# Hash attention with a gated feed-forward: head pairs, exponentials as the stationary operand, a feature-major hash in column tiles, token-major outputs

## Chip, cores and metric

One core of one Trainium2 chip. The metric is the device time of one execution in microseconds (us). Each kernel was executed four to eight times per batch, always beside the kernel before on the same chip. Most executions of one kernel agree within 1.5%; one that is over 1.5% above the fastest of its kernel is marked slow, and only the others ("fast runs") are compared. The clock in this text is the TensorE clock that the profile records as granted, as a share of full speed; in the records it is 1.0 or 0.5, and other values are means over a stretch. At full clock matmuls of 512 columns start 216 ns apart, or some 2.4 columns a nanosecond (written 2.4 GHz below).

## The reference, cut to what matters

```python
q, k, v: [4, 8, 768, 64] * 0.1      # batch, heads, sequence, head dimension
proj:    [64, 6]                    # hash projection
q_bits = (q @ proj > 0);  k_bits = (k @ proj > 0)          # 6 bits each
mask   = bucket(q_bits)[:, :, :, None] == bucket(k_bits)[:, :, None, :]
scores = where(mask, q @ k^T / 8, -1e9)
attn   = softmax(scores);  attn_out = attn @ v
x      = attn_out as [3072, 512]
ffn    = (gelu(x @ w_gate) * (x @ w_val)) @ w_out          # w_gate, w_val: [512, 1536]
out    = x + sigmoid(x @ w_res) * ffn
```

Both kernels compute the mask inside the score matmul: the 64 features of a query or key get hash rows appended, so that a mismatch in a bit makes the score so negative that its exponential vanishes.

## The kernel before, the parts that matter

```python
# per head and side: transposes, hash, signs, transposed back as rows
for t in range(ST):
    nc.tensor.transpose(ap[:D, bass.ts(t, 128)], ten_s[:, t, :], ident)          # L104, fp32
for (n0, nsz) in NCH:                                                            # (0, 512), (512, 256)
    nc.scalar.copy(ten_aug[0:D, n0:n0 + nsz], ap[:D, n0:n0 + nsz])               # L106
for t in range(ST):
    nc.tensor.matmul(bp[:, t * NBITS:(t + 1) * NBITS],
                     ten_aug[0:D, bass.ts(t, 128)], proj_sb, ...)                # L109: loads 128 columns, streams 6
nc.scalar.activation(sgn[:, :], bp[:, :ST * NBITS], AF.Sign)
for t in range(ST):
    nc.tensor.transpose(sp[:NBITS, bass.ts(t, 128)], sgn[:, t, :], ident_bf)     # L116
nc.scalar.copy(ten_aug_bf[D:KAUG, :], sp[:NBITS, :S])                            # L117
# ... cut ...
# per head: values stationary, exponentials streamed; output is feature-major
for jt in range(ST):
    for (n0, nsz) in NCH:
        sp = score_psum.tile([128, 512], FP32, tag="sp")                         # 2 single-bank buffers
        nc.tensor.matmul(sp[:, :nsz], k_aug_bf[0:KAUG, bass.ts(jt, 128)],
                         q_aug_bf[0:KAUG, n0:n0 + nsz], ...)                     # L134
        nc.scalar.activation(e[:, n0:n0 + nsz], sp[:, :nsz], AF.Exp,
                             scale=exp_scale, bias=exp_bias_sb)                  # L138
    for (ot, n0, nsz) in ots:
        nc.tensor.matmul(ot[:, :nsz], v_aug[:, jt, :], e[:, n0:n0 + nsz], ...)   # L141
for (ot, n0, nsz) in ots:
    nc.vector.reciprocal(recip[0:1, n0:n0 + nsz], ot[D:D + 1, :nsz])             # L148: one partition
nc.gpsimd.partition_broadcast(recip[:, :], recip[0:1, :])
# ... x = ot * recip, then: weights loaded and cast, feed-forward,
#     feature-major output transposed back to rows (L222, L223) ... cut ...
```

The softmax here doesn't subtract the row's maximum and nothing guards it: scores larger than these inputs give would overflow.

## Time and profile before

| | before |
|---|---|
| time, four executions of the batch that timed the change | median 800.62 us (793.58 to 805.14) |
| span of the profiled execution | 793.3 us |
| attention (to about 535 us), mean clock | 0.66 from 24 to 533 us |
| feed-forward with weight load and tail | about 258 us |

The groups by shape that the change touches, beyond the views that the prediction quotes (line, engine, operation, out<-in, shapes, count | busy us, mean ns of one | idle time of the engine just before, and what ended it):

```profile
L138 ACT ACTIVATE e<-sp,exp_bias_sb 128x512 bf16<-128x512 f32 x192 | 131.9, 687 | 61.6 <-PE sp L134 57.3 <-PE ap L104 0.7
L148 DVE RECIPROCAL recip<-ot 1x512 f32<-1x512 f32 x32 | 107.3, 3352 | 141.9 <-PE ot L141 141.9
L141 PE MATMUL ot<-e,v_aug 128*65 128x512 bf16 x192 | 104.2, 543 | 26.8 <-ACT e L138 26.8
L109 PE MATMUL bp<-proj_sb,q_aug 64*128 64x6 f32 x384 | 71.7, 316 | 1.5 <-ACT q_aug L106 1.5
```

The hash group L109 (twice: this one for queries, a like one for keys) streams six columns per matmul. The profile lists every fp32 matmul except transposes as two records, so the 768 records of L109 are 384 matmuls of the program; no sum here depends on it. A reciprocal of one partition takes 3.35 us for 512 columns. These 32 take 107 us of VectorE, and 162 us with the 32 of 256 columns (54.8 us, not shown), though most of it beside other work.

### The profile page before, as it was taken

Reading aid. Unit: us, or ns where it says so; the run is one execution under the profiler, and the core shown is the slowest. Engines: PE = TensorE matmul, PEld = TensorE weight load, DVE = VectorE, ACT = ScalarE, POOL = GpSimd, SP = SyncE. Lnnn points to the kernel's source line nnn. Section 1 sums busy time; section 2 is a strip of 40 time slices with the busy share of each in tenths; the row PEclk is TensorE's granted clock in tenths of the full one; section 3 lists DMA queues with packets and bytes.
Section 4 is the critical chain, followed back from the end, with each engine's and each line's share of the span. In section 5 each row is a group of like instructions: output and inputs, shape, how many; then the busy total and the mean of one; then the engine's idle time right before and its main releaser. Section 6 shows DMA issues by size and latency. Waiting matters only on the chain.

```text
span 793.3 us, 8913 instructions
## 1 busy us (share of the span) xinstructions
PE 712.2 (90%) x3360; PEld 412.1 (52%) x3360; DVE 325.4 (41%) x383; ACT 409.0 (52%) x845; POOL 37.5 (5%) x40
## 2 busy tenths in 40 slices
PE   3999998899998899998899998773889999999995
PEld 3666665566665566665556664330334444444442
DVE  1033434633346554444564335545524243333331
ACT  1465556755567675556665655550333343445341
POOL 0000000100001010000100000010000000000000
PEclk9965557865567785557675655555899999999997
DMA  8211111111111121111111000008531010101001
GB/s 141 58 40 41 40 41 30 41 41 40 40 40 39 32 51 40 40 41 30 40 31 31 0 1 1 0 0 283 154 85 61 1 54 0 54 12 43 32 22 54
DMA packets 82299, 36.24 MB, mean 46 GB/s; under 512 B 76112, under 2 KB 76112, under 8 KB 82256
## 3 DMA queue, kind: packets, MB, share of 16 engines
q1 hardware_dynamic: 82256, 35.66, 17.3%
q8 instruction: 27, 0.44, 0.2%
q14 instruction: 16, 0.13, 0.1%
HBM read 29.36 MB, written 6.29 MB: 45 GB/s over the span
## 4 chain that ended last, share of the span: by engine, by line
PE 78%; ACT 10%; issue 6%; DMA 4%; DVE 2%; ACTq 0%; POOL 0%; DVEq 0%; POOLq 0%
PE bp L109 17%; PE ot L141 13%; PE ap L104 10%; PE sp L134 10%; PE fps L213 7%; PE gps L191 7%; PE vps L197 7%; ACT e L138 5%; PE sp_raw L116 5%; DMA tmp<-in_moe_w_out_dram 3%; PE rps L205 2%; ACT k_aug_bf L117 2%; DMA out_dram<-o_row 1%; PE tp L222 1%; ACT q_aug_bf L117 1%
## 5 line engine op out<-in xcount | busy, mean ns | idle before, releaser
L138 ACT ACTIVATE e<-sp,exp_bias_sb 128x512 bf16<-128x512 f32 (+1 forms) x384 | 206.8, 577 | 61.6 <-PE sp L134 57.3
L148 DVE RECIPROCAL recip<-ot 1x512 f32<-1x512 f32 x64 | 160.9, 2532 | 141.9 <-PE ot L141 141.9
L141 PE MATMUL ot<-e,v_aug 128*65 128x512 bf16 (+1 forms) x384 | 166.4, 458 | 26.8 <-ACT e L138 26.8
L134 PE MATMUL sp<-q_aug_bf,k_aug_bf 70*128 70x512 bf16 (+1 forms) x384 | 153.6, 454 | 0.0
L194 ACT ACTIVATE gtmp<-gps 128x512 bf16<-128x512 f32 x72 | 42.9, 597 | 109.8 <-PE gps L191 109.2
L191 PE MATMUL gps<-x_sb,t 128*128 128x512 bf16 x288 | 81.0, 392 | 11.4 <-DVE t L169 9.8
L134 PEld LDWEIGHTS <-k_aug_bf 70*128 70x128 bf16 x384 | 50.3, 131 | 71.8 <-issue 61.3
L197 PE MATMUL vps<-x_sb,t 128*128 128x512 bf16 x288 | 78.5, 389 | 5.8 <-DVE t L169 5.8
L109 PEld LDWEIGHTS bp<-proj_sb,q_aug 64*128 64x128 f32 x384 | 68.8, 271 | 17.5 <-ACT q_aug L106 17.1
L199 DVE TENSOR_TENSOR hh<-gtmp,vps 128x512 bf16<-128x512 bf16 x72 | 49.3, 687 | 69.1 <-PE vps L197 59.9
L141 PEld LDWEIGHTS <-v_aug 128*65 128x65 bf16 x384 | 56.4, 147 | 38.9 <-issue 23.5
L109 PE MATMUL bp<-proj_sb,q_aug 64*128 64x6 f32 x384 | 71.7, 316 | 1.5 <-ACT q_aug L106 1.5
L109 PEld LDWEIGHTS bp<-proj_sb,k_aug 64*128 64x128 f32 x384 | 61.1, 244 | 17.7 <-ACT k_aug L106 17.7
L213 PE MATMUL fps<-hh,t 128*128 128x512 bf16 x288 | 64.7, 382 | 4.3 <-DVE t L169 4.2
L109 PE MATMUL bp<-proj_sb,k_aug 64*128 64x6 f32 x384 | 64.0, 296 | 1.6 <-ACT k_aug L106 1.6
L112 ACT ACTIVATE sgn_t<-bp 128x36 bf16<-128x36 f32 x64 | 12.8, 200 | 94.6 <-PE bp L109 94.6
L149 POOL PARTITION_BROADCAST recip<-recip x32 | 36.4, 1137 | 495.6 <-DVE recip L148 495.6
L104 PE MATMUL ap<-ident,q_s 128*64 128x128 f32 x192 | 46.7, 403 | 14.5 <-POOL ident masks.py:199 9.0
L121 DVE CAST k_aug_bf<-k_aug 64x768 bf16<-64x768 f32 x32 | 18.0, 562 | 83.4 <-ACT k_aug L106 83.4
L191 PEld LDWEIGHTS <-t 128*128 128x128 bf16 x288 | 27.6, 100 | 43.0 <-issue 8.8
L104 PE MATMUL ap<-ident,k_s 128*64 128x128 f32 x192 | 46.7, 405 | 3.4 <-ACT q_aug_bf L117 3.4
L197 PEld LDWEIGHTS <-t 128*128 128x128 bf16 x288 | 27.9, 99 | 40.8 <-DVE t L169 10.1
(34 smaller groups left out, 473.0 us busy)
## 6 DMA issues: line engine op xcount, KB each, us to landing
q_s<-in_q_dram SPq DMA_DIRECT2D x32, 192.0 KB, 2.6
k_s<-in_k_dram SPq DMA_DIRECT2D x32, 192.0 KB, 2.6
v_tmp<-in_v_dram SPq DMA_DIRECT2D x32, 192.0 KB, 3.0
out_dram<-o_row SPq DMA_DIRECT2D x24, 256.0 KB, 2.0
tmp<-in_moe_w_gate_dram SPq DMA_DIRECT2D x4, 768.0 KB, 4.2
tmp<-in_moe_w_val_dram SPq DMA_DIRECT2D x4, 768.0 KB, 4.2
tmp<-in_moe_w_out_dram SPq DMA_DIRECT2D x12, 256.0 KB, 2.7
tmp<-in_moe_w_res_dram SPq DMA_DIRECT2D x4, 256.0 KB, 2.7
```

The costliest lines, as they stand in the source:

```text
L104: nc.tensor.transpose(ap[:D, bass.ts(t, 128)], ten_s[:, t, :], ident)
L109: nc.tensor.matmul(bp[:, t * NBITS:(t + 1) * NBITS], ten_aug[0:D, bass.ts(t, 128)], proj_sb, start=True, stop=True)
L116: nc.tensor.transpose(sp[:NBITS, bass.ts(t, 128)], sgn[:, t, :], ident_bf)
L134: nc.tensor.matmul(sp[:, :nsz], k_aug_bf[0:KAUG, bass.ts(jt, 128)], q_aug_bf[0:KAUG, n0:n0 + nsz], start=True, stop=True)
L138: nc.scalar.activation(e[:, n0:n0 + nsz], sp[:, :nsz], AF.Exp, scale=exp_scale, bias=exp_bias_sb)
L141: nc.tensor.matmul(ot[:, :nsz], v_aug[:, jt, :], e[:, n0:n0 + nsz], start=(jt == 0), stop=(jt == ST - 1))
L148: nc.vector.reciprocal(recip[0:1, n0:n0 + nsz], ot[D:D + 1, :nsz])
L191: nc.tensor.matmul(gps, wg[:, kk, bass.ts(m, P)], x_bf[:, kk, :], start=(kk == 0), stop=(kk == KM - 1))
L194: nc.scalar.activation(gtmp, gps, AF.Gelu)
L197: nc.tensor.matmul(vps, wv[:, kk, bass.ts(m, P)], x_bf[:, kk, :], start=(kk == 0), stop=(kk == KM - 1))
L199: nc.vector.tensor_mul(hh[:, m, :], gtmp, vps)
L213: nc.tensor.matmul(fps, wo[:, kk, bass.ts(m, P)], hh[:, kk, :], start=(kk == 0), stop=(kk == KF - 1))
```

## The change

Its intent: take the narrow matmuls out of attention and make every output come out in the layout that its consumer wants.

- Two heads share one fp32 transpose. The hash becomes one wide fp32 matmul per side and half, with the projection stationary and the tokens streamed; the four sides of two pairs write to four column tiles (partitions 0, 32, 64, 96). A comparison gives the bits, and small transfers copy them under the features.
- Scores of 1024 columns (two banks, filled from head and key tiles without gaps) get one exponential. The exponentials are the stationary operand of the value matmul: 65 columns are streamed (64 values and a one for the sum), and tokens come out in partitions. A reciprocal is then 128 x 6. One matmul per head adds a tiny epsilon times the sum of all values, for rows without a match.
- Feed-forward weights are loaded during attention and cast on GpSimd. The last matmuls use the hidden tile as the stationary operand, so rows come out ready to store. The sigmoid becomes a tanh.

```diff
-                    for t in range(ST):
-                        nc.tensor.matmul(bp[:, t * NBITS:(t + 1) * NBITS],
-                                         ten_aug[0:D, bass.ts(t, 128)], proj_sb, ...)
-                    nc.scalar.activation(sgn[:, :], bp[:, :ST * NBITS], AF.Sign)
-                    ... sign transposes, copy of the rows ...
+            for (t0, n) in CH:
+                hs = misc_ps.tile([P, 512], FP32, tag="m", name="hs")
+                for pi in range(2):
+                    for side in range(2):
+                        j = 2 * pi + side
+                        nc.tensor.matmul(hs[32 * j:32 * j + 32, :n * P], projw,
+                                         t32[pi, side][:, t0 * P:(t0 + n) * P], ...)      # L166
+                nc.vector.tensor_scalar(bits[:, t0 * P:(t0 + n) * P], hs[:, :n * P], 0.0, cst,
+                                        op0=ALU.is_gt, op1=ALU.add)                       # L169
... preparation of a pair's side: transposes L137, evacuation L139, casts to the two heads:
+                    nc.gpsimd.tensor_copy(ag[0:D, :, 0, :], t3[0:D])                      # L144
+                    nc.vector.tensor_copy(ag[0:D, :, 1, :], t3[D:2 * D])                  # L145
... value copies L150 and sums L154 to L157 on GpSimd ...
-                        nc.tensor.matmul(ot[:, :nsz], v_aug[:, jt, :], e[:, n0:n0 + nsz], ...)
+                sp = sc_ps.tile([P, 1024], FP32, tag="sp", name="sp")                     # 2 buffers of two banks
+                ... score matmuls into sp ...                                             # L212
+                e = e_pool.tile([P, 1024], BF16, tag="e", name="e")
+                nc.scalar.activation(e, sp, AF.Exp, scale=float(ALPHA))                   # L217
+                        nc.tensor.matmul(o, eps_sb, vsum[...], start=True, stop=False)    # L223
+                        for qt in range(qt0, qt0 + nq):
+                            nc.tensor.matmul(av[hi][:, qt, :], e[:, off:off + P],
+                                             va[:, hi, jt, 0:D + 1], ...)                 # L230
-                    nc.vector.reciprocal(recip[0:1, n0:n0 + nsz], ot[D:D + 1, :nsz])
-                nc.gpsimd.partition_broadcast(recip[:, :], recip[0:1, :])
+                nc.vector.reciprocal(rec, o[:, :, D])                                     # L201
... feed-forward ...
-                nc.scalar.activation(res[:, m, :], rps, AF.Sigmoid)
+                nc.scalar.activation(th, rps, AF.Tanh, scale=0.5)
+                    nc.tensor.matmul(fps, hh[:, m, bass.ts(tt, P)], wo[:, m, :], ...)
-            ... 16 transposes and 16 copies per row tile, then the store ...
+                nc.sync.dma_start(out_t[row // T, row % T], o)
```

## The prediction

> **What bounds the kernel now.** I read the page first (engines, slices, chain), then the groups by shape, then stretches and the order of time.
>
> ```profile
> PE 712.2 (90%) x3360; PEld 412.1 (52%) x3360; DVE 325.4 (41%) x383; ACT 409.0 (52%) x845; POOL 37.5 (5%) x40
> PEclk9965557865567785557675655555899999999997
> PE 78%; ACT 10%; issue 6%; DMA 4%; DVE 2%; ACTq 0%; POOL 0%; DVEq 0%; POOLq 0%
> PE bp L109 17%; PE ot L141 13%; PE ap L104 10%; PE sp L134 10%; PE fps L213 7%; PE gps L191 7%; PE vps L197 7%; ACT e L138 5%; PE sp_raw L116 5%; DMA tmp<-in_moe_w_out_dram 3%; PE rps L205 2%; ACT k_aug_bf L117 2%; DMA out_dram<-o_row 1%; PE tp L222 1%; ACT q_aug_bf L117 1%
> ```
>
> TensorE is the bound, and for two thirds of the span it runs at a granted clock of 0.5 to 0.8. The costliest line of the chain is not attention: it is the hash projection L109, 17% of 793 us = 135 us, for 768 matmuls of six columns. Transposes L104 (79 us) and sign transposes L116 (40 us) are preparation too.
>
> By stretches of time (columns: stretch, its length, busy us of PE, PEld, DVE, ACT, POOL with counts, clock, DMA share, GB/s):
>
> ```profile
> 160.00:220.00 60.00, 58.48 (x286) 39.29 (x285) 22.94 (x27) 34.92 (x72) 3.25 (x3) 0.61 0.18 40
> 460.00:535.00 75.00, 63.06 (x222) 32.91 (x222) 34.48 (x31) 41.57 (x82) 5.24 (x5) 0.52 0.00 0
> 535.00:565.00 30.00, 13.25 (x34) 3.57 (x35) 16.05 (x19) 3.56 (x5) 1.56 (x1) 0.54 0.71 237
> 615.00:780.00 165.00, 163.59 (x798) 75.39 (x796) 53.84 (x76) 67.27 (x145) 0.00 (x0) 1.00 0.07 26
> 780.00:793.00 13.00, 3.69 (x19) 1.49 (x17) 1.92 (x2) 3.47 (x16) 0.00 (x0) 0.68 0.22 82
> ```
>
> So: attention to 535 us; some 17 us of idle PE from 535 to 565 while feed-forward weights load and are cast; feed-forward at full clock from about 565 to 780; a tail of 13 us, transposing and storing the last rows.
>
> The order of time gives what one matmul really costs, from start to start (durations of single matmuls overlap):
>
> ```profile
> 63.11 0.80 PE L116 MATMUL sp_raw<-ident_bf,sgn_t 128*6 128x128 bf16 x6
> 64.79 1.49 PE L104 MATMUL ap<-ident,q_s 128*64 128x128 f32 x6
> 66.07 0.85 PE L141 MATMUL ot<-e,v_aug 128*65 128x512 bf16 x2
> 66.71 0.85 PE L134 MATMUL sp<-q_aug_bf,k_aug_bf 70*128 70x512 bf16 x2
> 67.49 2.73 PE L109 MATMUL bp<-proj_sb,q_aug 64*128 64x6 f32 x12
> ...
> 76.76 0.50 PE L116 MATMUL sp_raw<-ident_bf,sgn_t 128*6 128x128 bf16 x6
> ```
>
> At clock 0.5 (64 to 74 us), 768 columns of scores take 66.71 to 67.35 = 0.64 us, twelve hash matmuls 2.65 us, six transposes 64.79 to 66.07 = 1.28 us, or 213 ns each. At clock 1.0 (76 to 77.7 us) the sign transposes fall from 122 to 56 ns (single starts in the trace), while fp32 transposes take 213 ns in both stretches. Feed-forward matmuls of 512 columns at full clock are 216 ns apart.
>
> **What the Trainium skill says.**
> - "TensorE: Matmul & The Clock Gate", Part 1: the clock is half or full, set by activity in windows of about 3.4 us, and an idle window brings it down. The trace agrees on two levels and on 3.4 us pieces. But PE has no idle of that length at 160 to 220 us (58.5 busy of 60) and the clock still falls; it falls after windows holding twelve L109 matmuls, which load weights and stream almost nothing. I read the gate as counting streamed columns: counting starts per window, it rises after windows with at most one L109 record (about 90% streaming at half clock) and falls at full clock below about 60%. In the attention tail (500 to 533 us) PE streams 1.28 us of a 1.85 us period, 69%, and the clock stays at 0.5 throughout.
> - Same page, "Weight-path perf modes": loads of 128 bf16 columns get a fast path. The trace shows only that such a load hides behind a 128-column matmul: output transposes L222 come as close as 55 ns.
> - Same page, Part 3: small-M matmuls in different column tiles run concurrently; 2.38x was measured for three. No run here shows it yet.
> - "ScalarE: Activation LUTs", "What ACT_TABLE_LOAD costs": each pointer operand adds about 93 ns. The trace agrees: 512 columns take 687 ns with the bias pointer (L138), 597 ns without (L194).
>
> **The change part by part.** I take attention, feed-forward and edges apart.
>
> *Hash and preparation.* Removed: 768 L109, 384 L116, half of 384 transposes (two heads share one), and ScalarE copies L106, L112 and L117. On the chain that was 135 + 40 + 40 us of PE and some 30 us of ACT. Added: 192 transposes at 213 ns = 41 us; 64 fp32 hash matmuls. At four cycles per fp32 column (estimate: 128 columns in 213 ns at 2.4 GHz), one group of two pairs is 4 x 768 x 4 cycles = 5.1 us serial, 1.3 us if column tiles run together; at half clock twice that. Over eight groups: 10 to 82 us; I take concurrency, mixed clock, 16 us. VectorE evacuates each of 32 sides: 0.69 + 0.41 (sizes of L153) + 0.56 (L121) = 1.66 us, 53 us in all, beside PE.
>
> *Scores.* Same columns: 147,456, or 61 us at full and 123 at half clock.
>
> *Values.* Was 384 matmuls streaming 147,456 columns; becomes 1152 pairs of a 128-column load and 65 streamed columns, plus 32 epsilon matmuls of 390 columns (8 us). 65 columns alone are 27 ns, the load bounds it: I take 60 ns at full clock (the 55 of L222 plus a little), up to 108 at half. That is 69 to 124 us: no saving in itself.
>
> *Exponentials.* 384 become 144 of 1024 columns; slope (687 - 466)/256 = 0.863 ns, so 597 + 512 x 0.84 = 1.02 us each, 147 us instead of 207.
>
> *Period of a chunk of 1024 scores.* Full clock: PE 1024/2.4 = 0.43 + 8 x 0.06 = 0.91 us, ACT 1.02. Two score buffers: after an exponential ends come 8 value matmuls, the scores of two chunks later, some 0.25 us of latency, then the next exponential: (0.91 + 0.25 + 1.02)/2 = 1.1 us. Half clock: 0.85 + 8 x 0.108 = 1.72 us, PE-bound. I expect a mix weighted somewhat to full, 1.35 us: 144 x 1.35 = 195 us.
>
> *Attention sum.* Start 30 us (identity 9 us; the instruction order puts an epsilon matmul waiting on GpSimd, then both first groups' transposes and hashes, ahead of the first score). Chunks 195. Preparation between chunks: 24 sides x 1.28 = 31, hash 12, epsilon 8, final transposes 96 x 0.08 = 8, waits on two PSUM buffers 10, less 14 that fills ACT-bound slack = 55. Together 280 us, against 535.
>
> *Feed-forward.* 960 matmuls unchanged: 960 x 216 ns = 207 us. Weights are loaded during attention (GpSimd casts), so the 17 us of idle go. Token-major output removes 96 transposes, 96 ScalarE casts and five of six table-load pairs (the built order has one load per function), and shortens the tail from 13 to some 5 us. Entry 5 (last x transposes, one half-clock window), tail 5, stray waits 3: 220 us.
>
> Sum 280 + 220 = 500 us, 37% less.
>
> **The rivals.**
> 1. *The clock stays at half in attention.* For it: 69% streaming did not raise it; half-clock value/score chunks stream (853 + 8 x 54)/1720 = 75%. Against it: no L109 remains, and transposes and hashes come in dense clusters. Then 144 x 1.72 = 248, start 30, preparation 75: 353 + 220 = 573 us.
> 2. *Full clock and pipelined loads.* ACT-bound at 1.1 us: 30 + 158 + 37 + 218 = 443 us.
> 3. *Column tiles run one after another.* For it: only one source says otherwise, and not for fp32. 6 groups x 4 to 8 us more: 525 to 550 us.
> 4. *GpSimd becomes the bound:* per group four casts, value copies and sums, three weight casts: estimated 13 us of the 33 us a group has. Nothing in this trace times such an operation; if they took three times as long, groups would take 40 us, total 555.
>
> **Range and chances.** Rivals 1 and 2 bracket it: half the mass lies between 470 and 530; 3 and 4 would move it up, pipelined loads down. I take 445 to 560 for 8 in 10. Even the worst sum stays 25% below the kernel before, so faster is near certain: 0.985, within 2% 0.01, slower 0.005.
>
> **What would show it.** Group rows: exponentials of 128x1024 x144 near 1020 ns; reciprocals near 0.2 us instead of 3.35; two to three table loads in all. Stretches: feed-forward 210 to 220 us at clock 1.0, PE idle under 5 us before it. Starts of value matmuls 55 to 65 ns apart at full clock, about 108 at half; a mean clock in attention between 0.6 and 0.9. Hash matmuls of four tiles starting nearly together. Wrong if value pairs cost well over 110 ns, if the clock sits at 0.5, or if ACT waits on GpSimd or on the row copies of the hash.

## The result, and the profile after

The changed kernel took 422.03 us (median of four, 418.96 to 423.37), against 800.62 us for the kernel before on the same chip. The ratio is 0.529, with a 95% interval from 0.525 to 0.532. Ratios here are the mean time of one kernel's fast runs over that of the other's in the same rounds, so not quite the ratio of the medians. The result is correct. The prediction was 500 us with a range of 445 to 560: the direction was right, the size wrong, and the measured time lies below the range.

The page of the kernel after (engines, clock by slices, chain by engine):

```profile
PE 381.9 (91%) x2924; PEld 199.4 (47%) x2944; DVE 184.3 (44%) x315; ACT 200.2 (48%) x242; POOL 101.2 (24%) x157
...
PEclk9999999999999699999899999999999999999999
...
PE 67%; ACT 10%; DVE 8%; DMA 5%; issue 4%; POOL 3%; SPq 2%; ACTq 0%; DVEq 0%; POOLq 0%
```

The clock is at 90% or more in all slices but two. By stretches (the same columns as in the prediction), attention between its first and last exponential, and feed-forward:

```profile
31.50:206.00 174.50, 154.94 (x1886) 93.51 (x1884) 83.45 (x162) 140.35 (x144) 79.35 (x109) 0.98 0.42 142
209.40:421.10 211.70, 206.36 (x938) 93.62 (x955) 82.59 (x120) 58.59 (x97) 0.00 (x0) 0.99 0.08 30
```

The groups that answer to those before:

```profile
L217 ACT ACTIVATE e<-sp 128x1024 bf16<-128x1024 f32 x144 | 140.4, 1021 | 63.6 <-PE sp L212 59.4
L201 DVE RECIPROCAL rec<-av 128x6 f32<-128x6 f32 x32 | 6.1, 192 | 54.9 <-PE av L230 54.9
L230 PE MATMUL av<-va,e 128*128 128x65 bf16 x1152 | 61.7, 196 | 14.5 <-ACT e L217 10.5
L166 PE MATMUL hs<-t,projw 128*32 128x512 f32 x64 | 10.1, 708 | 2.6 <-DVE t L139 2.5
```

The exponentials cost the 1021 ns that were expected, the reciprocals 192 ns. The mean of a value matmul, 196 ns, says little, because matmuls overlap. The order of time says more (TensorE and ScalarE of the kernel after, steady chunks at full clock):

```profile
59.54 7.11 ACT L217 ACTIVATE e<-sp 128x1024 bf16<-128x1024 f32 x7
...
61.73 0.42 PE L230 MATMUL av<-va,e 128*128 128x65 bf16 x8 [0.26 <-ACT e L217]
...
61.99 0.59 PE L212 MATMUL sp<-aug,aug 71*128 71x512 bf16 x2
...
62.64 0.42 PE L230 MATMUL av<-va,e 128*128 128x65 bf16 x8
...
62.90 0.60 PE L212 MATMUL sp<-aug,aug 71*128 71x256 bf16 x3
```

Eight value matmuls, each with its own 128x128 load, take 61.73 to 61.99, or 0.26 us; single starts in the trace are 29 to 39 ns apart. The prediction had 60 ns. One of the two short falls of the clock shows the same at half clock:

```profile
140.30 0.64 PE L230 MATMUL av<-va,e 128*128 128x65 bf16 x8
140.75 1.04 PE L212 MATMUL sp<-aug,aug 71*128 71x512 bf16 x2
141.68 0.62 PE L230 MATMUL av<-va,e 128*128 128x65 bf16 x8
```

Here the starts are 54 to 57 ns apart, which is 65 columns at 1.2 GHz: the array is bound by what it streams, and the load is hidden. A chunk then takes some 1.3 us instead of the predicted 1.72, nearly all of it streaming, and the clock is back at full after 7 us.

Where exponentials do wait, it is preparation. The stretch from 76 us, in order of time:

```profile
76.92 1.84 DVE L145 CAST aug<-t 64x768 bf16<-64x768 f32 x1
76.96 0.82 PE L137 MATMUL tp<-ident,ld 128*128 128x128 f32 x6
77.35 0.99 POOL L154 TENSOR_TENSOR v<-ldv 128x384 f32<-128x384 f32 x1
...
78.68 1.01 DVE L139 TENSOR_SCALAR t<-tp 128x512 f32<-128x512 f32 x2
...
79.41 0.88 PE L137 MATMUL tp<-ident,ld 128*128 128x128 f32 x6 [1.00 <-DVE t L139]
79.72 0.56 DVE L145 CAST aug<-t 64x768 bf16<-64x768 f32 x1
...
80.85 1.94 ACT L217 ACTIVATE e<-sp 128x1024 bf16<-128x1024 f32 x2 [2.61 <-PE sp L212]
81.12 1.50 PE L166 MATMUL hs<-t,projw 128*32 128x512 f32 x16
```

The VectorE cast L145 takes 0.56 us alone but 1.84 us beside GpSimd's two-input sum L154. The evacuation L139 comes after it, the transposes at 79.41 wait for that, the scores stand behind the transposes, and ScalarE is idle for 2.61 us. Six transposes take 0.66 us here (109 ns each), not the 213 ns of the prediction. The eight hash matmuls of a group, sixteen records, take 1.50 us.

**Terms of the sum, measured.** The mean step from one exponential to the next, of the 121 steps under 1.5 us, is 1.018 us. At full clock most of them alternate between 0.92 us (the next exponential follows without a wait) and 1.11 us (it waits for scores), so two chunks take 2.03 us.

| term | predicted us | measured us | how it is measured |
|---|---|---|---|
| start | 30 | 31.5 | first exponential |
| 144 chunks | 195 | 147 | 144 x 1.018 |
| preparation between chunks | 55 | 28 | 206.0 - 31.5 - 147 |
| feed-forward with entry and tail | 220 | 215 | 421.1 - 206.0 |
| sum | 500 | 421 | |

Nearly all of the miss of 79 us lies in two terms of attention: 48 us in the chunks and 27 us in the preparation between them. Feed-forward adds 5 us and the start takes 1.5 away.

### The profile page after: what moved, and what is told of

Same layout as the page of the kernel before. It is cut to its first block, busy times and chain, and to the rows that moved or that the text cites. A ratio compares the mean times of both kernels' runs of the same rounds, so it can differ in the third digit from the quotient of the medians.

```text
span 421.1 us, 7282 instructions
## 1 busy us (share of the span) xinstructions
PE 381.9 (91%) x2924; PEld 199.4 (47%) x2944; DVE 184.3 (44%) x315; ACT 200.2 (48%) x242; POOL 101.2 (24%) x157
## 4 chain that ended last, share of the span: by engine, by line
PE 67%; ACT 10%; DVE 8%; DMA 5%; issue 4%; POOL 3%; SPq 2%; ACTq 0%; DVEq 0%; POOLq 0%
PE gps L276 15%; PE vps L282 15%; PE fps L294 15%; ACT e L217 10%; PE sp L212 6%; PE av L230 5%; PE rps L288 5%; DVE t L139 3%; DVE aug L145 3%; PE tp L137 3%; DMA wtmp<-in_moe_w_out_dram 2%; PE hs L166 2%; DMA ld<-in_k_dram 2%; DMA ld<-in_q_dram 1%; SPq L176 1%
## 5 line engine op out<-in xcount | busy, mean ns | idle before, releaser
L217 ACT ACTIVATE e<-sp 128x1024 bf16<-128x1024 f32 x144 | 140.4, 1021 | 63.6 <-PE sp L212 59.4
L212 PE MATMUL sp<-aug,aug 71*128 71x256 bf16 (+1 forms) x384 | 86.9, 332 | 0.0
L279 ACT ACTIVATE gt<-gps 128x512 bf16<-128x512 f32 x72 | 43.0, 597 | 88.5 <-PE gps L276 85.1
L284 DVE TENSOR_TENSOR hh<-gt,vps 128x512 bf16<-128x512 bf16 x72 | 49.5, 687 | 74.0 <-PE vps L282 67.0
L230 PE MATMUL av<-va,e 128*128 128x65 bf16 x1152 | 61.7, 196 | 14.5 <-ACT e L217 10.5
L276 PE MATMUL gps<-x_sb,wg 128*128 128x512 bf16 x282 | 73.9, 383 | 0.3
L282 PE MATMUL vps<-x_sb,wv 128*128 128x512 bf16 x283 | 73.2, 379 | 0.3
L230 PEld LDWEIGHTS <-e 128*128 128x128 bf16 x1152 | 46.3, 99 | 53.7 <-ACT e L217 49.0
L294 PE MATMUL fps<-wo,hh 128*128 128x512 bf16 x281 | 65.5, 379 | 0.4
L139 DVE TENSOR_SCALAR t<-tp 128x512 f32<-128x512 f32 x64 | 32.8, 550 | 28.1 <-PE tp L137 24.8
L144 POOL CAST aug<-t 64x768 bf16<-64x768 f32 x32 | 33.9, 1063 | 45.1 <-DVE t L139 24.9
L145 DVE CAST aug<-t 64x768 bf16<-64x768 f32 x32 | 28.9, 904 | 2.6 <-PE sp L212 1.7
L288 PE MATMUL rps<-wr,x_sb 128*128 128x512 bf16 x94 | 25.1, 387 | 0.3 <-issue 0.2
```

The source lines that it names most:

```text
L139: nc.vector.tensor_scalar_mul(tt[:, c0 * P:(c0 + n) * P], ps[:, :n * P], (1.0 / C) if side == 0 else 1.0)
L145: nc.vector.tensor_copy(ag[0:D, :, 1, :], t3[D:2 * D])
L212: nc.tensor.matmul(sp[:, off:off + nq * P], ks[hi][:, bass.ts(jt, P)], qs[hi][:, qt0 * P:(qt0 + nq) * P], start=True, stop=True)
L217: nc.scalar.activation(e, sp, AF.Exp, scale=float(ALPHA))
L230: nc.tensor.matmul(av[hi][:, qt, :], e[:, off:off + P], va[:, hi, jt, 0:D + 1], start=False, stop=(jt == T - 1), skip_group_check=True)
L276: nc.tensor.matmul(gps, wg[:, kk, bass.ts(m, P)], xr[:, kk, :], start=(kk == 0), stop=(kk == KM - 1))
```

## The experiments

Eighteen kernels ran, in five batches, each with three timed rounds. The median of the kernel before in these batches was 798.5 to 803.9 us. As the batches ran on different chips, a difference from the kernel after is given as the difference of the two ratios times 800 us.

### 1. The wide hash alone, in the kernel before

Question: does the clock fall because of the narrow hash matmuls? The kernel before keeps everything but the hash.

```diff
-                    for t in range(ST):
-                        nc.tensor.matmul(bp[:, t * NBITS:(t + 1) * NBITS],
-                                         ten_aug[0:D, bass.ts(t, 128)], proj_sb, ...)
-                    nc.scalar.activation(sgn[:, :], bp[:, :ST * NBITS], AF.Sign)
-                    ... six sign transposes and the copy of the rows ...
+                    for (n0, nsz) in NCH:
+                        nc.tensor.matmul(hp_raw[:NBITS, n0:n0 + nsz], proj_sb,
+                                         ten_aug[0:D, n0:n0 + nsz], ...)
+                    nc.scalar.activation(ten_aug_bf[D:KAUG, :], hp_raw[:NBITS, :S], AF.Sign)
```

> The kernel before, with one thing changed: the hash projection streams the 768 tokens past the stationary 64x6 projection (two wide fp32 matmuls per side) instead of loading the tokens as weights and streaming six columns; the sign is taken feature-major, so the sign transposes L116 and their copies go too. No column tiles, no head pairs. Theory (the clock fell because the narrow hash matmuls load and hardly stream): mean granted clock before the feed-forward rises from about 0.65 to over 0.85, attention becomes ScalarE-bound (per head about 6 x 1.08 us of exponentials, 1.9 of copies, 1.6 of signs: 10 us x 32 = 320 us), total 600 to 680 us. Rival (the clock depends on something else, such as small transposes or waits): PE time of the hash is the same at half clock (768 x 4 cycles at 1.2 GHz = 2.56 us against 2.65), only the sign transposes go (64 x 0.73 = 47 us), clock stays near 0.65, total 740 to 770 us.

Measured: 649.46 us (one of four slow), ratio 0.813 (0.802 to 0.825). Attention by stretch, first the kernel before, then this one:

```profile
24.00:533.00 509.00, 474.04 (x2251) 302.65 (x2250) 230.45 (x242) 311.07 (x630) 34.82 (x31) 0.66 0.14 32
```

```profile
23.00:384.00 361.00, 313.07 (x1380) 130.22 (x1380) 226.94 (x242) 290.73 (x569) 37.34 (x31) 0.94 0.20 45
```

Without a change in scores, exponentials or values, the clock goes from 0.66 to 0.94, and 150 us go (0.187 x 800). TensorE was more idle than before (48 of 361 us against 35 of 509), so idleness is not what had held the clock down. Part of the 150 us is the clock and part the removed instructions (the sign transposes and their copies go too), and this run does not separate them; runs 9 and 10 test narrow matmuls alone.

### 2 and 3. A slower value matmul, with and without more streaming

```diff
                         for qt in range(qt0, qt0 + nq):
+                            nc.tensor.matmul(av[hi][:, qt, 0:4], e[:, off:off + P],      # run 3: 0:65
+                                             zer[:, 0:4], start=False, stop=False, ...)
                             nc.tensor.matmul(av[hi][:, qt, :], e[:, off:off + P], ...)
```

> The changed kernel, with each of the 1152 value matmuls preceded by a second load of the same 128 columns and four columns of zeros, added to the same accumulator: the result stays right, and a value pair costs about what the prediction assumed (60 ns at full clock), with the extra time in loading, not streaming. Theory 1 (attention is bound by ScalarE, 1.02 us a chunk, and the clock stays up as long as about half of a window streams): chunk on PE 0.43 + 0.5 = 0.93 us, still under 1.02, clock over 0.95, time up by 0 to 15 us (422 to 437). Rival (the prediction's own chain: load-bound pairs would have lowered the clock): clock in attention 0.5 to 0.8, time 470 us or more.

Measured: 437.86 us, ratio 0.550 (0.544 to 0.556), 17 us more than the kernel after, at the upper edge of what theory 1 allowed.

> As a_load2, but the added matmuls stream 65 zero columns instead of four, so the value work is doubled in loads and streaming alike. Theory 1: time within 15 us of the changed kernel, and within 5 us of a_load2 if load and stream each take about 30 ns; clock over 0.95. If streaming share matters to the clock at this level, a_stream2 is faster than a_load2 in spite of doing more work. If TensorE bounds attention after all, both are 1152 x 30 ns = 35 us slower or more.

Measured: 448.91 us, ratio 0.563 (0.559 to 0.568), 28 us more, at clock 1.0. That lies between the theories, which had allowed 15 us at most or 35 us at least.

The first run puts the cost of a value matmul near the 60 ns that the prediction took: the two matmuls together start every 55 ns at full clock, where the single one starts every 29 to 39. So 128 more loaded and 4 more streamed columns add some 25 ns, which bounds the cost of such a load at full clock. Attention of it:

```profile
29.40:220.40 191.00, 179.04 (x3030) 119.77 (x3027) 85.06 (x162) 143.71 (x144) 80.04 (x109) 0.99 0.38 130
```

The clock stays at 0.99, and the steps under 1.5 us have a mean of 1.10 us. That is the 1.1 us of the prediction's full-clock formula, and a total near its rival 2. So even with nearly 60 ns the time would not have been 500. The mis-sized pair was worth 17 us; the half-clock share of the chunks, which did not come, was the larger error.

### 4. Exponentials of 512 columns

```diff
-                nc.scalar.activation(e, sp, AF.Exp, scale=float(ALPHA))
+                for i in range(2):
+                    nc.scalar.activation(e[:, i * 512:(i + 1) * 512],
+                                         sp[:, i * 512:(i + 1) * 512], AF.Exp, scale=float(ALPHA))
```

> The changed kernel with each 1024-column exponential split in two of 512 (288 instead of 144), nothing else: the wide exponentials undone alone. If ScalarE bounds attention: 288 x about 0.52 (0.597 less an overlap) to 0.6 us = 150 to 172 us instead of 147, of which the earlier release of half a chunk gives a little back: 5 to 25 us slower. If another engine bounds it: within 5 us.

Measured: median 426.73 us (two of its four executions, at 430 us and clock 0.955, are marked slow), ratio 0.529 from the fast ones (0.520 to 0.538). The kernel after has 0.529. Within this noise (some 8 us) the width of the exponential adds nothing: back to back, exponentials of 512 columns start 477 ns apart though each takes 597, so two take 0.95 us, where those of 1024 start 0.92 us apart though each takes 1.02.

### 5, 11, 13, 14. The old orientation of values, in the kernel after

Run 5 puts back the old attention core: values stationary, one tile of 768 scores at a time, feature-major accumulators, one-partition reciprocals with a broadcast. The hash, the preparation and the feed-forward stay as after. The edit, cut:

```diff
-                sp = sc_ps.tile([P, 1024], FP32, tag="sp", name="sp")
+                    sp = sc_ps.tile([P, 512], FP32, tag="sp", name="sp")       # 2 buffers
-                            nc.tensor.matmul(av[hi][:, qt, :], e[:, off:off + P], va[...], ...)
+                        nc.tensor.matmul(ot[:, :nsz], va[:, hi, jt, 0:D + 1], e[:, n0:n0 + nsz], ...)
-                nc.vector.reciprocal(rec, o[:, :, D])
+                    nc.vector.reciprocal(recip[0:1, n0:n0 + nsz], ot[D:D + 1, :nsz])
+                nc.gpsimd.partition_broadcast(recip[:, :], recip[0:1, :])
```

> The changed kernel with the attention core of the kernel before: values stationary, exponentials streamed, narrow exponentials of 512 and 256, one-partition reciprocals, GpSimd broadcast; hash, head pairs, preloaded weights and the new feed-forward stay. (x_tok is then made by as many transposes as x_sb was.) Theory: TensorE streams about as much as before the undoing, but the reciprocals alone are 32 x 5.07 = 162 us of VectorE, with preparation (some 75 us) and the final multiplies (35 us) about 270 us, so VectorE becomes the bound of attention: total 490 to 540 us at a clock over 0.85. Rival (the orientation of the value matmul does not matter beyond TensorE's columns): within 20 us of the changed kernel, 422 to 445.

Measured: 605.17 us, ratio 0.758 (0.751 to 0.764): 183 us more than the kernel after, and far above what was expected. Apart from its reciprocals, the orientation was believed to be nearly neutral. Two suspicions followed. The first was the reciprocals, replaced by a copy (a result that is wrong):

```diff
-                    nc.vector.reciprocal(recip[0:1, n0:n0 + nsz], ot[D:D + 1, :nsz])
+                    nc.vector.tensor_copy(recip[0:1, n0:n0 + nsz], ot[D:D + 1, :nsz])
```

> Wrong result on purpose: a_valfm with the two one-partition reciprocals of each head replaced by copies of the same shape (5.05 us of VectorE become about 1.1 us), to tell the cost of the normalization from that of the orientation. If the reciprocals are what made a_valfm slow (they hold VectorE and with it the accumulators and the preparation): 605 falls to 460 to 520 us. If the orientation itself and its narrow exponentials are: it stays above 570.

Measured: 614.48 us, ratio 0.766. No gain, so this theory fell. What both traces show on GpSimd is a wait of another kind (run 5):

```profile
216.32 1.98 POOL L218 PARTITION_BROADCAST recip<-recip  x2 [5.88 <-issue]
225.36 0.45 POOL L158 TENSOR_TENSOR v<-v 128x128 f32<-128x128 f32 x1 [7.06 <-issue]
```

Every change from a two-input sum to the broadcast, or back, has a configuration instruction ahead of it and mostly 5.7 to 8.0 us in which the profile shows nothing on GpSimd: some 190 us for 26 changes in the trace of run 5. It is a side effect of our experiment, as neither the kernel before nor the kernel after alternates the two. With the sums on VectorE it is gone:

```diff
-                nc.gpsimd.tensor_add(v3, vs[:, :, 0:3, :], vs[:, :, 3:6, :])
+                nc.vector.tensor_add(v3, vs[:, :, 0:3, :], vs[:, :, 3:6, :])
                 # and the other two sums likewise
```

> a_valfm with the three sums of v moved from GpSimd to VectorE, so that GpSimd has no two-input sum left beside the partition broadcast. Theory (each change between the two kinds costs GpSimd 6 to 7.6 us in which the accumulators wait for their broadcast): GpSimd's waits of that length vanish and the time falls from 605 to 480 to 540 us, VectorE then being the bound (reciprocals 162 us). Rival (orientation and narrow score buffers alone): above 580 us.

Measured: 584.97 us (two of four slow), ratio 0.727 (0.717 to 0.737). The switches had cost some 25 us; 158 us remain. Taking the reciprocals away from this form (wrong again):

> Wrong result on purpose: a_valsum with the reciprocals replaced by copies, as before in a_valfm_norecip. If VectorE's reciprocals bound a_valsum: 30 to 80 us faster than a_valsum. If the chain of two 512-column score buffers bounds it: within 10 us of a_valsum.

Measured: 569.37 us, ratio 0.715 (0.709 to 0.721): some 10 us, hardly more than the noise of the two. So neither of the two suspicions explains the orientation by itself. The clock fell as well (0.74 in attention, 0.81 in run 13), which may hide a part of the gain. Runs 17 and 18 return to it.

### 6. The old feed-forward, after the new attention

```diff
-    wload = (load_w(moe_w_gate, ...) + ...)         # issued during attention, cast on GpSimd
+        wg = load_w(moe_w_gate, DMODEL, DFF, "wg")   # after attention, cast on VectorE
     ... and the old feature-major residual, sigmoid, product, output transposes and copies
```

> The changed kernel with the old feed-forward: weights loaded and cast after attention, feature-major output, output transposes, sigmoid. The kernel before took 258 us from the end of attention to the end, the changed one 212: theory, 455 to 475 us (45 us more, from the wait for weights, one half-clock stretch, 96 transposes and the tail). Rival (weights hide behind the end of attention once attention has slack): under 440.

Measured: 457.36 us, ratio 0.572 (0.568 to 0.576): 34 us more: the time is in the expected range, the difference below the 45 us that were expected. Loading the weights earlier and the new layout are undone together here, so their shares are not known.

### 7. The hash in pieces, tile after tile

```diff
-                        nc.tensor.matmul(hs[32 * j:32 * j + 32, :n * P], projw,
-                                         t32[pi, side][:, t0 * P:(t0 + n) * P], ...)
+                        for c in range(n):
+                            nc.tensor.matmul(hs[32 * j:32 * j + 32, bass.ts(c, P)], projw,
+                                             t32[pi, side][:, bass.ts(t0 + c, P)], ...)
```

> The changed kernel with the hash matmuls cut in 128-column pieces and ordered so that four (or two) in a row use the same column tile: same columns, same results, column tiles hardly beside each other. If the tiles of one group run together only when neighbours differ: hash per group from 1.43 us to 4 to 5 us, 8 groups, 20 to 29 us more PE; time up by 8 to 30 us (430 to 452), since part falls into TensorE's slack under ScalarE. If order does not matter (concurrency was not what made it short): within 4 us.

Measured: 431.54 us, ratio 0.539 (0.536 to 0.543), 8 us more. Pieces of one column tile run one after another, 109 ns apart, and neighbouring tiles still overlap in part: a group takes 2.90 us instead of 1.50, not the 4 to 5 that were expected. In the kernel after, the four tiles of one step start within 20 ns and run together, as the prediction assumed.

### 8. An earlier first score

```diff
+                        if g < 2:   # first two groups: ScalarE evacuates the transposes
+                            nc.scalar.mul(tt[:, c0 * P:(c0 + n) * P], ps[:, :n * P], ...)
     ... the epsilon matmul goes to the end of a head, and prep(g + 1) after the first pair of g
```

> A new version: the changed kernel with ScalarE, idle then, evacuating the transposes of the first two groups, the epsilon matmul moved to the end of each head so that TensorE need not wait for GpSimd's sums at the start, and the next group's preparation placed after the first pair. Theory (the first 31.5 us without an exponential lie on the path): first exponential at 20 to 25 us, total 410 to 418. Rival (what is gained at the start is lost in the waits for preparation later): within 4 us of 422.

Measured: 420.35 us, ratio 0.526 (0.522 to 0.529), not clear of the kernel after, and outside the 410 to 418 of the theory. The first exponential comes at 25.1 us instead of 31.5, but most of what that wins is lost in waits later. A start gained is not worth its length while preparation sets the gaps.

### 9 and 10. Narrow against wide work of the same size

Two kernels add work to the preparation of every side, the results of which nobody reads. Run 9 adds 12 matmuls that load 128 columns and stream six; run 10 adds wide ones with about the same TensorE time at full clock.

```diff
+                    dm = misc_ps.tile([P, 512], FP32, tag="m", name="dm")
+                    for c in range(12):                                   # run 9: a_narrow
+                        nc.tensor.matmul(dm[:, c * NBITS:(c + 1) * NBITS],
+                                         t32[pi, side][:, bass.ts(c % T, P)], projw[:, 0:NBITS], ...)
+                        # run 10, a_wide: two matmuls per half instead,
+                        # nc.tensor.matmul(dm[0:32, :n * P], projw, t32[pi, side][:, t0 * P:(t0 + n) * P], ...)
```

> The changed kernel with work added whose result is thrown away: per pair and side, twelve narrow fp32 matmuls like those of the old hash (128 tokens loaded as weights, six columns streamed), 32 x 12 in all, 24 x 112 ns = 2.7 us of TensorE per pair and side at full clock. Theory (windows full of narrow matmuls bring the clock down, and nothing else does): clock before the feed-forward falls below 0.9, time at least 20 us above a_wide. Rival (the new kernel's clock is safe whatever little streams): clock as in a_wide, within 8 us of it.

> The control of a_narrow: the same TensorE time at full clock, but streamed: per pair and side the 768 columns twice past the 32-column projection in fp32 (1536 x 4 cycles at 2.4 GHz = 2.56 us). 32 x 2.56 = 82 us more TensorE work in an attention that has some 20 to 40 us of slack there: 470 to 505 us, clock over 0.97.

Measured: 582.84 us (ratio 0.728, 0.723 to 0.732) and 500.65 us (ratio 0.624, 0.622 to 0.625), both of the same chip. A stretch of attention of run 9, then of run 10:

```profile
100.00:200.00 100.00, 95.66 (x782) 73.94 (x783) 27.21 (x50) 37.42 (x39) 27.43 (x39) 0.74 0.24 86
```

```profile
100.00:200.00 100.00, 93.21 (x838) 49.34 (x839) 39.68 (x74) 51.81 (x55) 36.05 (x52) 0.98 0.30 95
```

TensorE is busy for 96 and 93 of 100 us, yet the clock is 0.74 in one and 0.98 in the other. At full clock the added work is about equal: 768 records 112 ns apart are 86 us in run 9, and 256 records of 430 and 215 ns are 83 us in run 10. But 70% of the narrow ones start 213 ns apart, at half clock. The 83 us between the two runs are the price of the same TensorE time spent on loads and not on streaming. With run 1 this settles the mechanism on which the prediction rested: the clock follows what is streamed.

### 12. The VectorE cast moved to GpSimd

Run 8 plus:

```diff
-                    nc.vector.tensor_copy(ag[0:D, :, 1, :], t3[D:2 * D])
+                    if g == 0: nc.vector.tensor_copy(ag[0:D, :, 1, :], t3[D:2 * D])
+                    else:      nc.gpsimd.tensor_copy(ag[0:D, :, 1, :], t3[D:2 * D])
```

> A new version: n_start with VectorE's cast of the second head moved to GpSimd from the second group on. In the profile of the changed kernel that cast takes 0.56 us alone and up to 2.3 us beside a two-input GpSimd sum, and the transposes then wait for VectorE. Theory (these waits make up a good part of the 34 us in which ScalarE stands between exponentials): gaps fall below 25 us, time 405 to 415. Rival (GpSimd, at some 20 of 22 us per group, becomes the bound): 425 or more.

Measured: 419.46 us, ratio 0.521 (0.519 to 0.524), smaller than expected. The stretched cast is gone, but the idle time between exponentials hardly falls (34 us between the first and the last in the kernel after, 33 us here), so the cast was not what set it.

### 15, 16. Four or three single-bank score buffers

Run 12 plus scores and exponentials of 512 columns; run 16 gives one bank to preparation instead.

```diff
-        sc_ps = actx.enter_context(tc.tile_pool(name="sc_ps", bufs=2, space=PSUM))   # of 2 banks
+        sc_ps = actx.enter_context(tc.tile_pool(name="sc_ps", bufs=4, space=PSUM))   # of 1; run 16: 3
-            for c in range(0, len(bk), 2):   # 1024 scores, one exponential
+            for c in range(len(bk)):         # 512 scores, one exponential
```

> A new version: n_pool with scores in four single-bank buffers of 512 columns and one exponential per bank (288), in place of two of 1024 columns. Theory (the chain exponential, values, scores, exponential over two buffers sets 1.015 us per 1024 columns; back to back ScalarE would need 2 x 0.493): 3 to 8 us faster than n_pool, 410 to 416 us. Rival (more, smaller waits): within 3 us or slower.

> n_sc4 with one bank moved from the scores (three) to preparation (three instead of two). If preparation's two banks cause the waits of 1 to 2.7 us between exponentials, these shrink and it is 3 to 10 us faster than n_sc4; if three score banks are too few, it is slower.

Measured: 411.36 us, ratio 0.515 (0.508 to 0.522), and 414.08 us (two of four slow), ratio 0.515 (0.508 to 0.521), both correct. Run 16 is no faster than run 15, so a third bank for preparation does not pay for the lost score bank. ScalarE of run 15 over 7 us of steady chunks:

```profile
98.72 6.49 ACT L224 ACTIVATE e<-sp 128x512 bf16<-128x512 f32 x13
105.55 0.60 ACT L224 ACTIVATE e<-sp 128x512 bf16<-128x512 f32 x1 [0.34 <-PE sp L219]
```

Thirteen exponentials follow each other without a wait, some 477 ns apart, so 1024 scores cost 0.95 us, where the alternating steps of run 12 (0.92 and 1.11) have a mean of 1.015. Over 144 chunks that would be 9 us. By the ratios the gain over run 12 is 5 us, with an uncertainty of 6, so its size is not shown. This is the fastest version that we have, 11 us or 2.6% below the kernel after by the ratios. The two were timed on different chips, each beside the kernel before, and their intervals lie 0.003 apart, so the order is likely and the size rough.

### 17. Two single-bank score buffers, token-major

```diff
-                sp = sc_ps.tile([P, 1024], FP32, tag="sp", name="sp")    # 2 of these: four banks
+                sp = sc_ps.tile([P, 512], FP32, tag="sp", name="sp")     # 2 of these: two banks
```

> The changed kernel with two score buffers of one bank (512 columns) instead of two of two banks, one exponential per bank; all else as in it. Chain: exponential 0.60, values 0.13, scores 0.21, latencies 0.25 = 1.19 us for two buffers of 512, so 1.19 us per 1024 columns against 1.015. Theory (the score banks are the value of the token-major form): 144 x 0.175 = 25 us more and longer waits behind preparation, since less is buffered: 450 to 490 us. Rival (orientation itself): under 440.

Measured: 472.84 us (two of four slow), ratio 0.594 (0.588 to 0.601): 52 us more than the kernel after. ScalarE at full clock:

```profile
99.54 1.09 ACT L216 ACTIVATE e<-sp 128x512 bf16<-128x512 f32 x2 [0.18 <-PE sp L211]
100.80 1.09 ACT L216 ACTIVATE e<-sp 128x512 bf16<-128x512 f32 x2 [0.18 <-PE sp L211]
102.07 1.09 ACT L216 ACTIVATE e<-sp 128x512 bf16<-128x512 f32 x2 [0.18 <-PE sp L211]
```

With two banks, ScalarE waits for scores in every pair of exponentials, and 1024 scores take 1.26 us at full clock (mean of the steps under 1.6 us, half clock included: 1.30) against 1.018. The clock in attention is 0.88 against 0.98, so a part of the 52 us is half clock.

### 18. The old orientation with four score banks

```diff
-        sc_ps = ...(name="sc_ps", bufs=2)
-        av_ps = ...(name="av_ps", bufs=2)
+        sc_ps = ...(name="sc_ps", bufs=4)
+        av_ps = ...(name="av_ps", bufs=1)
```

Run 13 is changed. It and the kernel after fill eight PSUM tiles of 512 fp32 columns (banks). A feature-major head has 768 columns of output and takes two of them, where a token-major head has 6 x 65 and takes one. So with four score banks and two for preparation only one set of accumulators is left.

> a_valsum with four score banks instead of two and single instead of double accumulators (two banks per head); eight exponential tiles let ScalarE run ahead of a waiting accumulator. Theory (score banks): 585 falls to 500 to 545 us, VectorE (some 270 us busy in attention) being next. Rival (single accumulators cost as much as the score banks gain, or orientation itself): 565 or more.

Measured: 626.67 us, ratio 0.788 (0.783 to 0.793): worse than with two banks, against the expectation. The exponentials of 512 columns, and then TensorE and ScalarE at the start of a head, show why:

```profile
L209 ACT ACTIVATE e<-sp 128x512 bf16<-128x512 f32 x192 | 119.6, 624 | 237.2 <-PE ot L212 159.5 <-PE sp L207 77.5
```

```profile
112.61 3.62 PE L212 MATMUL ot<-e,va 128*65 128x256 bf16 x11
113.12 1.64 ACT L209 ACTIVATE e<-sp 128x512 bf16<-128x512 f32 x4 [5.03 <-PE ot L212]
```

ScalarE waits 160 us for value matmuls (ot) to free its exponential tiles, because these wait for the accumulators, which wait for 5 us of reciprocals at the end of each head. The value matmuls of a head then run in one block, as the second view shows. Between the waits the step is 0.79 us per 768 scores (mean of the 136 steps under 1.8 us), or 1.05 per 1024. That looks as good as the token-major form, but 97 of the 136 steps hold no value matmul at all. It shows only that scores and exponentials alone keep this pace with four banks. Whether the old orientation would keep it with its value matmuls in between was not shown, since no run gives it four score banks and double accumulators (ten banks with those of preparation).

What run 13 lost can be counted. Its mean step was 1.324 us per 768 scores (the 158 under 1.8 us), and 192 of these are 254 us, against 147 us of the kernel after. The steps far above that, at head ends and preparation, add 67 us against 28. Together that is 146 us of the 153 us between the profiled executions (574.5 and 421.1 us). The causes of the 107 us of steady steps are less clear. Run 17 isolates one: with two score banks the token-major form takes 1.30 us per 1024 scores against 1.018, or 144 x 0.28 = 41 us. The other 66 us would be the value of filling banks without gaps (144 pairs of exponentials and not 192), if the two orientations were alike in all else. That is not shown: a third of the steps of run 13 (55 of 158) hold no value matmul, and at full clock these take 1.06 us and those with two or more 1.34 (medians). The clock, a mean of 0.81 in its attention against 0.98, is a small part of the steps: at full clock alone their mean is 1.26 us, or 12 us less in all. So the 66 us are an estimate, and no run isolates the packing from the orientation.

**What the parts are worth.** The hash took 150 us off the kernel before (run 1). Undone from the kernel after, the value part costs 158 us (run 13, without the GpSimd artefact) and the feed-forward 34 us (run 6). These add up to 342 of the 377 us between the two kernels (0.471 x 800). Their sum is a rough one, as one part is taken from the kernel before and two from the kernel after. The rest, 35 us, is left to what none of these runs undoes: head pairs in the transposes, casts that moved off ScalarE, and parts that depend on each other.

## Why the prediction was wrong, by its own steps

**What bounds it, and what to remove: right.** TensorE at a low clock was the bound, and the narrow hash was the worst of it (run 1). The clock follows streamed columns and not busy time (runs 1, 9, 10).

**Hash: right, in part by luck.** Four column tiles run together: 1.50 us per group measured, 1.3 estimated. Rival 3 was wrong. The four cycles per fp32 column were taken from transposes that take 213 ns at half clock, as if it were full. Transposes take two cycles per column, and it is luck that fp32 matmuls take four: in run 10 each of the two records of a 512-column matmul takes 430 ns at full clock.

**Exponentials, reciprocals: right.** 1021 ns against 1020; 192 ns against 0.2 us. The groups show x144.

**Values: the failed step.** "65 columns alone are 27 ns, the load bounds it: I take 60 ns at full clock (the 55 of L222 plus a little), up to 108 at half." L222 gave the distance of matmuls that stream 128 columns, and 128 columns at 2.4 GHz are 53 ns by themselves. That distance was therefore the streaming of that matmul, and it bounded the load from above only; the prediction read it as the load's cost. Measured: 29 to 39 ns at full clock and 54 to 57 at half, about the streaming of 65 columns. At full clock this was worth some 17 us (run 2).

**Period of a chunk: the larger part of the same failure.** "I expect a mix weighted somewhat to full, 1.35 us." The full-clock formula was good: with 60 ns it gives 1.1, and run 2, with 55 ns, measured 1.10. With 31 ns it gives (0.25 + 0.43 + 0.25 + 1.02) / 2 = 0.98, and 1.018 was measured. The half-clock share was wrong, for two reasons. First, the threshold: the prediction had the clock fall "below about 60%" of streaming, and at its own 1.1 us a chunk streams 0.64 of 1.1 us (1024 + 8 x 65 columns at 2.4 GHz), 58%, so it placed the steady chunk just on the falling side. Run 2 streams 0.66 of 1.10 us, 59%, and holds 0.99. Run 17 streams 0.64 of 1.26 us, 51%, and holds full clock through stretches of pure chunks, though it also falls now and then. By counting starts in windows of 3.41 us, those after which the kernel after fell in attention had 48% and 35%, and such falls of run 17, in windows without preparation, came after 47 to 52%. Second, the way back: at half clock a chunk takes 1.3 us and streams nearly all of it, so the clock rises again by itself, where the predicted 75% would not have raised it. In run 17, where a half-clock chunk takes 1.58 us and streams 81%, the clock stayed low for up to 20 us at a time. So the pair cost that was 17 us at full clock may also decide whether half clock can last. That is argued from these shares; no run shows it by itself, since run 2 spent only 3.4 us of its attention at half clock.

**Preparation: too large by 27 us.** Its main term, "24 sides x 1.28", used 213 ns per transpose "in both stretches". The second of these stretches ends at 77.7 us and holds no fp32 transposes; the next six start at 78.13 us, just after the record has gone back to half clock (78.08 us). So both readings were of half clock. Fp32 transposes are 109 ns apart at full clock and 213 at half, in the kernel after and in some places of the kernel before. That alone is 24 x 0.62 = 15 us. The rest of the difference is not split further. Waits for preparation were predicted and are there, and one contribution was not foreseen: the VectorE cast that stretches beside GpSimd sums. But taking it away (run 12) hardly shortened the gaps, and a third preparation bank (run 16) brought nothing over run 15, so what sets these gaps stays open.

**Start and feed-forward: right.** 31.5 against 30 us, and 215 against 220.

**Rivals.** Rival 2, full clock and pipelined loads, was the right one in kind and 21 us too high, by its 1.1 us chunk and its 37 us of preparation. Rival 1 did not come, rival 4 neither: GpSimd is busy for 79 of 174.5 us of attention. The prediction weighed rivals 1 and 2 alike. What separates them is the cost of a matmul of 65 columns behind a load of 128, and the streaming share that follows from it; the kernel before has no bf16 matmul that streams fewer columns than it loads, so its trace could not give that cost.

## What to carry to other kernels

Spacings of matmuls that stream as many columns as they load give only an upper bound for the load; look for a stream narrower than the load before pricing one, and otherwise carry both cases through to the end, because the price also sets the streaming share, and with it the clock. When matmuls are turned around, count the PSUM banks that each orientation needs for accumulators: here two score banks fewer cost 52 us with all else kept (run 17). A pace that is measured between waits can leave out the very work that is waited for (run 18), so count what runs inside the steps. A part that is undone for an experiment can bring a cost of its own (here GpSimd's switching), so look at its trace, and at its clock, before its time is called the value of the part.

## What the Trainium skill lacked or had wrong

- "TensorE: Matmul & The Clock Gate", Part 1 and the table of what matters: the clock is said to fall after an idle window, and to swing, without a figure, when there are frequent short pauses between groups. In the runs it falls on a busy TensorE that streams little: 0.74 with TensorE busy for 95.7 of 100 us (run 9), 0.98 with 93.2 of 100 (run 10). A figure in streamed columns is missing; here windows without preparation held full clock in run 17 with 53% or more of streaming, those of 47 to 52% sometimes lost it, and at half clock steps with 81% did not raise it (run 17) while nearly 100% did (kernel after).
- Same page, "Back-to-back issue gap": a load and matmul pair of 128 columns is given as 81 ns, and the simple formula of columns over the clock as an under-count for such pairs. The pairs here (128x128 load, 65 columns) start 29 to 39 ns apart at full clock and 54 to 57 at half, which the simple formula gives; transposes of 128 bf16 columns came as close as 55 ns.
- Same page, Part 4: no figure for fp32 transposes. They start 109 ns apart at full clock and 213 ns at half.
- Same page, Part 3: no measured figure for fp32, nor for four column tiles. Eight fp32 hash matmuls over four tiles take 1.50 us per group; in 128-column pieces ordered tile after tile, 2.90 us.
- "ScalarE: Activation LUTs", "What ACT_TABLE_LOAD costs": the overlap of activations back to back is given as 93 ns. With a free buffer ahead, exponentials of 512 columns start 477 ns apart and take 597 ns, an overlap of 120 ns; those of 1024 columns start 920 ns apart and take 1021, an overlap of 101 ns.
- "GPSIMD Engine Reference", Instruction dispatch: about 6 us are given for the first call after a load of a library. The runs show mostly 5.7 to 8.0 us between the two kinds of instruction, but the page does not say that alternating partition broadcast and two-input sums pays it every time: some 190 us of GpSimd time in run 5.
